# A linear-attention and token-mixing kernel: state update split over VectorE and GpSimd, mixing by single tiles and token pairs, weight flips ranked later, and a planner with larger latencies

## The chip, the cores and the metric

The kernel runs on one core of one Trainium2 chip. The metric is the device time of one execution in microseconds (us); lower is better. Fast runs of one kernel on one chip agree within about 1.5% here. The profile of the kernel before is of a run that the record marks slow (169.96 us, 0.1 us above the slowest fast run timed beside it). Ratios are the mean time of one kernel's fast runs over the mean of the other kernel's fast runs of the same rounds, so they are not quite the ratio of the medians that are quoted.

## The reference

Two stages follow each other. For each of 4 batches and 8 heads (768 tokens, head width 48) a recurrence runs over the tokens:

```python
for t in range(S):
    cur = einsum('bhd,bhe->bhde', u * k_t, v_t)
    y_t = einsum('bhd,bhde->bhe', r_t, state + cur)
    state = w[..., None] * state + einsum('bhd,bhe->bhde', k_t, v_t)
```

The result, as x with 384 channels per token, goes through a token-mixing layer:

```python
theta = x @ w_theta
yr = einsum('ts,bsd->btd', w_tok_r, x * cos(theta))
yi = einsum('ts,bsd->btd', w_tok_i, x * sin(theta))
u = x + yr + yi
out = u + maximum(u @ w_ch, 0)
```

The mixing of one output token needs all tokens s of its batch.

## The kernel before

The kernel records tasks first. A task has an engine, an expected duration, what it reads and writes, a priority and the PSUM banks that it takes. A list scheduler, run while the program is built, then fixes the order of the instructions on each engine. On the chip each engine works through its order and waits where data is late. The order depends on what the planner believes of delays:

```python
    def add(self, eng, ns, fn, rd=(), wr=(), prio=0.0, lat=60.0, ...):
        ...
    # in order(): a task has been chosen for engine e
                    free_at[e] = now + ns
                    t.end = now + ns + t.lat
                    ...
                    for x in t.users:
                        x.ready = max(x.ready, t.end)
```

The tokens are cut into 6 chunks of 128 per batch, worked in pairs (`pr`). The front of a batch turns r, k and v into scores, outputs and the running state. The state of chunk cc is made by four VectorE instructions, and GpSimd scales it to the bf16 operand of the next chunk:

```python
                    for hp in range(HP):
                        nc.vector.scalar_tensor_tensor(
                            Y[:, cc, hp, :], Y[:, cc - 1, hp, :], wC[:, hp:hp + 1],
                            src[:, hp], op0=Alu.mult, op1=Alu.add)
                ...
                P.add(POOL, ..., lambda cc=cc: nc.gpsimd.tensor_mul(Sb[:, cc], Y[:, cc], wide(wC, D)), ...)
```

The token weights are turned by TensorE (24 flips of three 128x128 blocks); ScalarE empties all 24 banks. The mixing takes two token tiles at a time, waits for all of the batch's zr and zi (`zk`), and flips both tiles together:

```python
        zk = [("zr", zj, o) for o in range(NCH)] + [("zi", zj, o) for o in range(NP)]
        for pr in range(NP):
            for t in range(2):
                for part in range(4):        # three matmuls each: WrT first, then WiT
                    P.add(PE, 495, mix, rd=zk + [...], ...)
                P.add(DVE, ..., un[:, t] = bank + x ...)
            flip6(uT ..., both tiles, ...)   # 6 transposes, one ScalarE eviction
            for t in range(2):
                P.add(PE, 495, chan, ...)    # channel matmuls
                P.add(DVE, ..., fin[:, t] = max(bank, 0) + un[:, t] ...)
            P.add(SP, 500, one output DMA for two tiles)
```

The fronts of later batches have higher priority than the mixing of earlier ones, so the mixing fills TensorE's gaps.

Of the kernel before, what the change touches and what calls it, by code (L numbers as in the profile page):

```python
# [29 lines left out]

class Task:
    __slots__ = ("eng", "ns", "fn", "deps", "prio", "seq", "lat", "acq", "uses", "nwait",
                 "users", "ready", "end", "mode")


class Plan:
# [9 lines left out]
    def add(self, eng, ns, fn, rd=(), wr=(), prio=0.0, lat=60.0, acq=(), use=(), mode=None):  # L46
        t = Task()
        t.eng, t.ns, t.fn, t.prio, t.lat, t.mode = eng, ns, fn, prio, lat, mode
# [23 lines left out]
    def order(self):  # L72
# [15 lines left out]
        while len(out) < n:  # L88
            for e in waiting:
                while free_at[e] <= now:  # L90
                    nfree = sum(1 for b in banks if b[0] <= now)
                    best = None
                    for t in waiting[e]:
                        if t.ready <= now and len(t.acq) <= nfree:
                            if best is None or (t.prio, t.seq) < (best.prio, best.seq):
                                best = t
# [13 lines left out]
                    t.end = now + ns + t.lat  # L110
# [6 lines left out]
                    for x in t.users:  # L117
                        x.ready = max(x.ready, t.end)
                        x.nwait -= 1
                        if x.nwait == 0:  # L120
                            waiting[x.eng].append(x)
# [19 lines left out]
def kernel(  # L141
# [63 lines left out]
    Ys = ring(1, [C, NS, HP, D], F32, "Y")  # L205
# [8 lines left out]
    uns = ring(2, [C, 2, HD], BF16, "un")  # L214
    uTs = ring(2, [C, 2, ND, C], BF16, "uT")
    fins = ring(2, [C, 2, HD], F32, "fin")
# [11 lines left out]
    def pool_ns(n):  # L228
        return 190 + 1.95 * n
# [112 lines left out]
    def token_weights(prio):  # L342
        for to in range(NCH):
            for src, dst, key in ((moe_w_tok_r, WrT, "WrT"), (moe_w_tok_i, WiT, "WiT")):
                i = load_rows(src[to * C:(to + 1) * C, :].rearrange("p (o c) -> p o c", o=2), 2)
                for sg in range(2):
# [10 lines left out]
                    def evac(sg=sg, tok=tok, dst=dst, to=to):  # L357
                        nc.scalar.activation(  # L358
                            dst[:, 3 * sg:3 * sg + 3, to * C:(to + 1) * C],
                            bank(tok)[:, :3 * C].rearrange("p (j c) -> p j c", j=3), Act.Copy)  # L360
                    P.add(ACT, act_ns(3 * C), evac, use=[tok], wr=[(key, to, sg)],
                          prio=prio + to)
# [15 lines left out]
    def front(b, base):  # L378
        Y, Sb = Ys[0], Sbs[b % 2]
        x, zr, zi = xs[b % 3], zrs[b % 2], zis[b % 2]  # L380
        xi, zj = b % 3, b % 2
        for pr in range(NP):
# [33 lines left out]
            for c in range(2):  # L416
# [12 lines left out]
                P.add(PE, 330, scores, rd=[kT, rT], acq=tk, prio=pb + 2, mode=1)  # L429
# [20 lines left out]
            P.add(ACT, 130, lambda td=td, dg=dg: nc.scalar.activation(  # L450
# [19 lines left out]
            for c in cs:  # L470
                cc = 2 * pr + c

                def update(cc=cc, c=c, ts=ts):
                    src = bank(ts)[:, c * HP * D:(c + 1) * HP * D].rearrange(
                        "p (h e) -> p h e", h=HP)
                    if cc == 0:
                        nc.vector.tensor_copy(Y[:, 0], src)
                        return
                    for hp in range(HP):
                        nc.vector.scalar_tensor_tensor(  # L480
                            Y[:, cc, hp, :], Y[:, cc - 1, hp, :], wC[:, hp:hp + 1],
                            src[:, hp], op0=Alu.mult, op1=Alu.add)
                P.add(DVE, 270 if cc == 0 else 480, update, use=[ts],
                      rd=["wC"] + ([("Y", cc - 1)] if cc else []), wr=[("Y", cc)], prio=pb + 2)
                P.add(POOL, pool_ns(HP * D), lambda cc=cc: nc.gpsimd.tensor_mul(  # L485
                    Sb[:, cc], Y[:, cc], wide(wC, D)),
                    rd=[("Y", cc), "wC"], wr=[("Sb", b % 2, cc)], prio=pb + 2)
# [29 lines left out]
            P.add(PE, 900, outputs, rd=[rT] + mk + [kv_] + [  # L517
# [14 lines left out]
            for t in range(2):  # L532
# [12 lines left out]
                P.add(ACT, act_ns(HD), lambda th=th: nc.scalar.activation(  # L545
# [5 lines left out]
            P.add(POOL, pool_ns(2 * HD), lambda sn=sn, pr=pr: nc.gpsimd.tensor_mul(  # L551
                zi[:, 2 * pr:2 * pr + 2], x[:, 2 * pr:2 * pr + 2], sn),
                rd=xk + [("sin", g % 2, t) for t in range(2)], wr=[("zi", zj, pr)], prio=pb + 9)


    def mixing(b, base):
        x, zr, zi = xs[b % 3], zrs[b % 2], zis[b % 2]
        xi, zj = b % 3, b % 2
        zk = [("zr", zj, o) for o in range(NCH)] + [("zi", zj, o) for o in range(NP)]
        for pr in range(NP):  # L560
            g = b * NP + pr
            un, uT, fin = uns[g % 2], uTs[g % 2], fins[g % 2]
            pb = base + 10 * pr
            for t in range(2):
                to = 2 * pr + t
                tm = ("mx", b, to)
                for part in range(4):
                    def mix(tm=tm, to=to, part=part):
                        WT, z = ((WrT, zr), (WiT, zi))[part // 2]
                        for j in range(3):  # L570
                            so = 3 * (part % 2) + j
                            nc.tensor.matmul(bank(tm)[:, :HD], WT[:, so, to * C:(to + 1) * C],  # L572
                                             z[:, so], start=(part == 0 and j == 0),
                                             stop=(part == 3 and j == 2))
                    P.add(PE, 495, mix, rd=zk + [(n, to, s) for n in ("WrT", "WiT") for s in (0, 1)],
                          acq=[tm] if part == 0 else [], use=[] if part == 0 else [tm],
                          wr=[] if part == 0 else [tm], prio=pb + 2 * t, mode=0)
                P.add(DVE, dve_ns(HD), lambda tm=tm, t=t, to=to, un=un: nc.vector.tensor_add(
                    un[:, t], bank(tm)[:, :HD], x[:, to]), use=[tm],
                    rd=[("x", xi, pr, hi) for hi in range(2)], wr=[("un", g % 2, t)],  # L580
                    prio=pb + 2 * t)
            flip6(uT.rearrange("p t d c -> p (t d) c"),
                  [un[:, t, dk * C:(dk + 1) * C] for t in range(2) for dk in range(ND)],
                  ("TU", b, pr), pb + 4, [("un", g % 2, t) for t in range(2)], [("uT", g % 2)])
            for t in range(2):
                tf = ("f", b, 2 * pr + t)

                def chan(tf=tf, t=t, uT=uT):
                    for dk in range(ND):
                        nc.tensor.matmul(bank(tf)[:, :HD], uT[:, t, dk, :], Wch[:, dk, :],  # L590
                                         start=(dk == 0), stop=(dk == ND - 1))
                P.add(PE, 495, chan, rd=[("uT", g % 2), ("Wch", 0), ("Wch", 2)], acq=[tf],
                      prio=pb + 4, mode=0)
                P.add(DVE, dve_ns(HD), lambda tf=tf, t=t, un=un, fin=fin:
                      nc.vector.scalar_tensor_tensor(fin[:, t], bank(tf)[:, :HD], 0.0, un[:, t],
                                                     op0=Alu.max, op1=Alu.add),
                      use=[tf], rd=[("un", g % 2, t)], wr=[("fin", g % 2, t)], prio=pb + 4)
            P.add(SP, 500, lambda fin=fin, pr=pr: nc.sync.dma_start(
                out=out[b, 2 * pr * C:(2 * pr + 2) * C, :].rearrange("(t p) n -> p t n", p=C),
                in_=fin), rd=[("fin", g % 2, t) for t in range(2)], wr=[("out", b, pr)],  # L600
                prio=-2e6, lat=2000)

    setup()
    square(moe_w_theta, Wth, "Wth", 20, 5.5)
    front(0, 0)
    token_weights(20)
# [39 lines left out]
```

## Time and profile before

| | before |
|---|---|
| time, median of 3 runs | 169.72 us (169.3 to 169.85) |
| span of the profiled run | 168.2 us |
| TensorE, VectorE, ScalarE, GpSimd busy | 136.4, 118.0, 90.0, 76.2 us |
| first mixing matmul starts | 49.9 us |
| batch 1's first outputs start (its matmuls with the scores) | 52.6 us |
| last theta group (the three theta matmuls of the last tile) starts | 136.1 us |

The page's lines of busy time in 40 equal slices (4.2 us each; a digit is tenths) show that the program has regimes:

```profile
PE   0354675999648997989979998989899899999960
...
DVE  2549369381479899997999699958999654443242
ACT  3673581999972766557953459327661481011110
...
PEclk9999997899999999999995999999999999999998
```

TensorE has gaps for the first third and hardly any in the last fifth; VectorE is fullest in the middle and thin in the last fifth. The same by window, with busy time and instruction count of each engine in each stretch:

```profile
0.00:53.00 53.00, 33.38 (x453) 26.75 (x453) 31.00 (x72) 36.08 (x67) 26.10 (x37) 0.97 0.98 244
30.00:45.00 15.00, 13.03 (x165) 11.38 (x164) 7.12 (x16) 15.00 (x36) 5.53 (x5) 0.98 1.04 288
53.00:136.50 83.50, 76.65 (x1019) 49.58 (x1014) 74.57 (x163) 47.97 (x79) 48.44 (x45) 0.98 0.54 119
136.50:168.20 31.70, 26.38 (x176) 15.36 (x174) 12.39 (x25) 5.93 (x10) 1.67 (x2) 0.98 0.20 76
```

The columns are the stretch, its length, then TensorE matmuls, weight loads, VectorE, ScalarE, GpSimd, then the granted TensorE clock, the DMA share and GB/s. TensorE idles 19.6 of the first 53 us and only 6.9 of the next 83.5. From 30 to 45 us ScalarE has no free moment. The chain of waits (start, length, what) in that stretch:

```profile
37.61 0.57 ACT WiT L358
...
39.88 0.67 ACT WrT L358
40.56 0.77 ACT WiT L358 x2
...
41.74 1.12 ACT WiT L358 x2
42.86 1.12 ACT Wch L338 x2
```

These are the weight evictions, L358.

### The profile page before, as it was taken

To read this page: it belongs to the slowest core of one execution; us is meant where nothing else is said; L and a number is where in the kernel's file an instruction comes from. 1 tells how busy PE (TensorE), PEld (TensorE's weight loads), DVE (VectorE), ACT (ScalarE), POOL (GpSimd) and SP (SyncE) were. 2 spreads that over 40 slices of the span, in tenths; PEclk is the share of its full clock that TensorE was granted. 3 is DMA by queue.
4 is the path that set the end of the run, shared out by engine and by line. 5 is a ranking of instruction groups with operands and counts; after the bars stand their busy time and mean duration, and the time that the engine had idled before them with its cause. 6 is when DMAs were issued, how large, how long until landed. Compare 5 with 4: busy or idle time off the path is not lost.

```text
span 168.2 us, 4181 instructions
## 1 busy us (share of the span) xinstructions
PE 136.4 (81%) x1641; PEld 91.7 (54%) x1641; DVE 118.0 (70%) x257; ACT 90.0 (53%) x155; POOL 76.2 (45%) x82
## 2 busy tenths in 40 slices
PE   0354675999648997989979998989899899999960
PEld 0243545879435655556765664556746555655530
DVE  2549369381479899997999699958999654443242
ACT  3673581999972766557953459327661481011110
POOL 6228247055298398927773774306517360000000
PEclk9999997899999999999995999999999999999998
DMA  4999999998999996099969972202200002220222
GB/s 88 222 236 218 214 264 383 410 339 172 180 215 208 194 207 124 0 228 194 243 167 213 218 156 44 97 2 93 97 0 4 0 4 93 93 77 17 97 95 93
DMA packets 80892, 25.25 MB, mean 150 GB/s; under 512 B 75368, under 2 KB 79336, under 8 KB 80872
## 3 DMA queue, kind: packets, MB, share of 16 engines
q1 hardware_dynamic: 80848, 24.98, 60.9%
q8 instruction: 13, 0.21, 0.5%
q14 instruction: 7, 0.06, 0.1%
q10 hardware_dynamic: 24, 0.00, 0.0%
HBM read 20.25 MB, written 4.72 MB: 148 GB/s over the span
## 4 chain that ended last, share of the span: by engine, by line
PE 38%; DVE 31%; ACT 15%; issue 6%; DMA 5%; POOL 2%; SPq 2%; DVEq 0%; POOLq 0%; ACTq 0%
PE bank_61 L572 3%; DVE Y_120 L480 3%; PE bank_66 L572 3%; DMA ld_86<-in_r_dram 3%; DVE Kw_98 L404 3%; PE bank_64 L572 2%; DMA ld_94<-in_r_dram 2%; PE bank_68 L572 2%; DVE PD_112 L437 2%; ACT KT_110 L373 2%; ACT WiT L358 2%; DVE zr_132 L548 2%; PE bank_63 L572 2%; ACT sin_136 L542 2%; DVE PD_113 L437 2%
## 5 line engine op out<-in xcount | busy, mean ns | idle before, releaser
L572 PEld LDWEIGHTS <-WrT 128*128 128x128 bf16 x144 | 14.0, 100 | 9.2 <-issue 0.9
L572 PEld LDWEIGHTS <-WiT 128*128 128x128 bf16 x144 | 12.9, 98 | 6.6
L485 POOL TENSOR_TENSOR Sb_122<-Y_120,wC 128x192 bf16<-128x192 f32 x10 | 6.1, 614 | 9.1 <-DVE Y_120 L480 8.4
L392 POOL TENSOR_TENSOR Rw_96<-ld_85,wpow 128x384 bf16<-128x384 f32 x6 | 5.9, 995 | 5.1 <-PE bank_67 L370 5.1
L485 POOL TENSOR_TENSOR Sb_121<-Y_120,wC 128x192 bf16<-128x192 f32 x10 | 5.7, 574 | 3.1 <-DVE Y_120 L480 2.3
L538 PEld LDWEIGHTS <-xT_138 128*128 128x128 bf16 x36 | 3.4, 107 | 5.6 <-ACT xT_138 L373 2.3
L551 POOL TENSOR_TENSOR zi_134<-x_129,sin_136 128x768 bf16<-128x768 bf16 x2 | 3.3, 1635 | 6.8 <-ACT sin_136 L542 6.8
L404 DVE TENSOR_TENSOR Kw_100<-ld_86,wpinv 128x384 bf16<-128x384 f32 x6 | 5.7, 963 | 0.0
L373 ACT ACTIVATE uT_143<-bank_62 128x768 bf16<-128x768 bf16 x2 | 1.6, 812 | 7.5 <-PE bank_62 L370 7.5
L392 POOL TENSOR_TENSOR Rw_95<-ld_94,wpow 128x384 bf16<-128x384 f32 x4 | 4.3, 1074 | 2.9 <-DMA ld_94<-in_r_dram 2.9
L373 ACT ACTIVATE uT_142<-bank_63 128x768 bf16<-128x768 bf16 x2 | 1.6, 811 | 7.1 <-PE bank_63 L370 7.1
L590 PEld LDWEIGHTS <-uT_143 128*128 128x128 bf16 x36 | 3.1, 98 | 4.1 <-ACT uT_143 L373 2.5
L548 DVE TENSOR_TENSOR zr_132<-bank_68,x_129 128x384 bf16<-128x384 f32 x3 | 1.7, 554 | 5.1 <-ACT bank_68 L545 2.7
L392 POOL TENSOR_TENSOR Rw_95<-ld_88,wpow 128x384 bf16<-128x384 f32 x4 | 4.7, 1188 | 1.0 <-PE bank_63 L370 1.0
L551 POOL TENSOR_TENSOR zi_134<-x_131,sin_136 128x768 bf16<-128x768 bf16 x2 | 3.3, 1636 | 3.9 <-ACT sin_136 L542 2.7
L538 PEld LDWEIGHTS <-xT_139 128*128 128x128 bf16 x36 | 3.1, 98 | 3.5 <-ACT xT_139 L373 1.9
L426 PEld LDWEIGHTS <-KT_111 64*128 64x128 bf16 x96 | 3.0, 101 | 3.6 <-ACT KT_111 L373 2.2
L426 PEld LDWEIGHTS <-KT_110 64*128 64x128 bf16 x96 | 3.1, 101 | 3.3 <-ACT KT_110 L373 2.3
L590 PEld LDWEIGHTS <-uT_142 128*128 128x128 bf16 x36 | 3.2, 97 | 3.1 <-ACT uT_142 L373 1.4
L551 POOL TENSOR_TENSOR zi_135<-x_130,sin_137 128x768 bf16<-128x768 bf16 x2 | 3.3, 1637 | 3.5 <-ACT sin_137 L542 3.2
L274 PE MATMUL bank_61<-ident_f,wu 8*128 8x8 f32 x1 | 0.2, 241 | 5.6 <-DMA wu<-in_u_dram 5.6
L437 DVE TENSOR_TENSOR PD_112<-RT_106,KT_110 128x1024 bf16<-128x1024 bf16 x3 | 2.6, 875 | 2.9 <-ACT KT_110 L373 2.9
(561 smaller groups left out, 504.4 us busy)
## 6 DMA issues: line engine op xcount, KB each, us to landing
out_dram<-fin_144 SPq DMA_DIRECT2D x6, 384.0 KB, 2.5
out_dram<-fin_145 SPq DMA_DIRECT2D x6, 384.0 KB, 2.8
ld_85<-in_r_dram SPq DMA_DIRECT2D x6, 192.0 KB, 4.3
ld_86<-in_k_dram SPq DMA_DIRECT2D x6, 192.0 KB, 3.6
ld_87<-in_v_dram SPq DMA_DIRECT2D x6, 192.0 KB, 3.5
ld_88<-in_r_dram SPq DMA_DIRECT2D x4, 192.0 KB, 4.4
ld_89<-in_k_dram SPq DMA_DIRECT2D x4, 192.0 KB, 4.6
ld_90<-in_v_dram SPq DMA_DIRECT2D x4, 192.0 KB, 3.6
```

The source lines that it names most:

```text
L373: P.add(ACT, act_ns(n * C), lambda: nc.scalar.activation(dst, bank16(tok)[:, :n * C].rearrange("p (a c) -> p a c", a=n), Act.Copy), use=[t ...
L392: lambda c=c, vec=vec, Rw=Rw, ir=ir: vec.tensor_mul(Rw[:, c, :, :D], Ls[ir][:, c * HD:(c + 1) * HD].rearrange("p (h d) -> p h d", h=H), wpow),
L404: P.add(DVE, dve_ns(HD), lambda c=c, Kw=Kw, ik=ik: nc.vector.tensor_mul(Kw[:, c, :, :D], Ls[ik][:, c * HD:(c + 1) * HD].rearrange("p (h d) ...
L426: nc.tensor.matmul(bank(tk[hi])[:, hp * C:(hp + 1) * C], KT[q, c, hp, :], RT[q, c, hp, :], start=(hp == 0), stop=(hp == HP - 1))
L437: nc.vector.tensor_mul(PD, RT, KT)
L480: nc.vector.scalar_tensor_tensor(Y[:, cc, hp, :], Y[:, cc - 1, hp, :], wC[:, hp:hp + 1], src[:, hp], op0=Alu.mult, op1=Alu.add)
L485: P.add(POOL, pool_ns(HP * D), lambda cc=cc: nc.gpsimd.tensor_mul(Sb[:, cc], Y[:, cc], wide(wC, D)), rd=[("Y", cc), "wC"], wr=[("Sb", b % ...
L538: nc.tensor.matmul(bank(th)[:, :HD], xT[:, t, dk, :], Wth[:, dk, :], start=(dk == 0), stop=(dk == ND - 1))
L548: P.add(DVE, dve_ns(HD), lambda th=th, to=to: nc.vector.tensor_mul(zr[:, to], bank(th)[:, :HD], x[:, to]), use=[th], rd=xk, wr=[("zr", zj, ...
L551: P.add(POOL, pool_ns(2 * HD), lambda sn=sn, pr=pr: nc.gpsimd.tensor_mul(zi[:, 2 * pr:2 * pr + 2], x[:, 2 * pr:2 * pr + 2], sn), rd=xk + [ ...
L572: nc.tensor.matmul(bank(tm)[:, :HD], WT[:, so, to * C:(to + 1) * C], z[:, so], start=(part == 0 and j == 0), stop=(part == 3 and j == 2))
L590: nc.tensor.matmul(bank(tf)[:, :HD], uT[:, t, dk, :], Wch[:, dk, :], start=(dk == 0), stop=(dk == ND - 1))
```

## The change

Its intent is to relieve VectorE of the state update and ScalarE of half the evictions, to let the mixing of a batch begin before its last pair is ready and drain tile by tile, to keep the weights from delaying the first batch, and to give the planner more realistic numbers. The diff, cut to its core:

```diff
+LATENCY = {PE: 200.0, DVE: 150.0, ACT: 175.0, POOL: 160.0, SP: 2200.0}
-    def add(..., lat=60.0, ...):
+        t.lat = LATENCY[eng] if lat is None else lat
-                    t.end = now + ns + t.lat
+                    done = now + ns
+                    t.end = done + t.lat
-                        x.ready = max(x.ready, t.end)
+                        x.ready = max(x.ready, done if x.eng == e else t.end)
 # ... state update
-                    for hp in range(HP):
-                        nc.vector.scalar_tensor_tensor(Y[:, cc, hp, :], ...)
+                        nc.vector.tensor_add(Ys[cc % 2], src, Zs[(cc - 1) % 2])
+                P.add(POOL, ..., nc.gpsimd.tensor_mul(Zs[cc % 2], Ys[cc % 2], wide(wC, D)))
+                P.add(ACT, ..., nc.scalar.activation(Sb[:, cc], Zs[cc % 2], Act.Copy))
 # ... weight evictions
-                        nc.scalar.activation(...)
+                        if sg: nc.vector.tensor_copy(o, i)
+                        else:  nc.scalar.activation(o, i, Act.Copy)
 # ... mixing: one tile at a time, three parts, each with the four matmuls of one token pair
+        for to in range(NCH):
+            for part in range(NP):
+                P.add(PE, 660, mix, rd=[(n, zj, 2 * part + j) for n in ("zr", "zi") for j in range(2)] + [...])
+            # then add, a flip of 3 blocks, channel matmuls, relu-add, output DMA for this tile
 # ... ranks
-    square(moe_w_theta, Wth, "Wth", 20, 5.5)
+    square(moe_w_theta, Wth, "Wth", 15, 8.5)
-    token_weights(20)
+    token_weights(60)
```

Some expected durations were corrected too, the planner no longer adds 100 ns for a change of TensorE mode around weight flips, zi is made per tile instead of per pair, and un, uT and fin rotate over three buffers.

More of the change, by code (lines that the diff above doesn't have):

```diff
@@ L28 @@
 PE, DVE, ACT, POOL, SP = "PE", "DVE", "ACT", "POOL", "SP"
+KEEP = 0
+LATENCY = {PE: 200.0, DVE: 150.0, ACT: 175.0, POOL: 160.0, SP: 2200.0}
 class Task:
     __slots__ = ("eng", "ns", "fn", "deps", "prio", "seq", "lat", "acq", "uses", "nwait",
-                 "users", "ready", "end", "mode")
+                 "users", "ready", "end", "mode", "keep")
 class Plan:
@@ L44, in __init__, with add @@
         self.bank_of = {}
-    def add(self, eng, ns, fn, rd=(), wr=(), prio=0.0, lat=60.0, acq=(), use=(), mode=None):
+    def add(self, eng, ns, fn, rd=(), wr=(), prio=0.0, lat=None, acq=(), use=(), mode=0, keep=0):
         t = Task()
-        t.eng, t.ns, t.fn, t.prio, t.lat, t.mode = eng, ns, fn, prio, lat, mode
+        t.eng, t.ns, t.fn, t.prio, t.mode = eng, ns, fn, prio, mode
+        t.keep = keep
+        t.lat = LATENCY[eng] if lat is None else lat
         t.seq = len(self.tasks)
@@ L93, in order @@
                     for t in waiting[e]:
-                        if t.ready <= now and len(t.acq) <= nfree:
+                        if t.ready <= now and (
+                                not t.acq or len(t.acq) + t.keep <= nfree):
                             if best is None or (t.prio, t.seq) < (best.prio, best.seq):
@@ L204 @@
     mATs = ring(6, [C, 2, HP, C], BF16, "mAT")
-    Ys = ring(1, [C, NS, HP, D], F32, "Y")
+    Ys = ring(2, [C, HP, D], F32, "Y")
+    Zs = ring(2, [C, HP, D], F32, "Z")
     Sbs = ring(2, [C, NS, HP, D], BF16, "Sb")
@@ L213 @@
     xTs = ring(2, [C, 2, ND, C], BF16, "xT")
-    uns = ring(2, [C, 2, HD], BF16, "un")
-    uTs = ring(2, [C, 2, ND, C], BF16, "uT")
-    fins = ring(2, [C, 2, HD], F32, "fin")
+    uns = ring(3, [C, HD], BF16, "un")
+    uTs = ring(3, [C, ND, C], BF16, "uT")
+    fins = ring(3, [C, HD], F32, "fin")
     Wth = sb.tile([C, ND, HD], BF16, name="Wth")
@@ L357, in evac @@
                     def evac(sg=sg, tok=tok, dst=dst, to=to):
-                        nc.scalar.activation(
-                            dst[:, 3 * sg:3 * sg + 3, to * C:(to + 1) * C],
-                            bank(tok)[:, :3 * C].rearrange("p (j c) -> p j c", j=3), Act.Copy)
-                    P.add(ACT, act_ns(3 * C), evac, use=[tok], wr=[(key, to, sg)],
-                          prio=prio + to)
+                        o = dst[:, 3 * sg:3 * sg + 3, to * C:(to + 1) * C]
+                        i = bank(tok)[:, :3 * C].rearrange("p (j c) -> p j c", j=3)
+                        if sg:
+                            nc.vector.tensor_copy(o, i)
+                        else:
+                            nc.scalar.activation(o, i, Act.Copy)
+                    P.add(DVE if sg else ACT, dve_ns(3 * C) if sg else act_ns(3 * C), evac,
+                          use=[tok], wr=[(key, to, sg)], prio=prio + to)
     def flip6(dst, blocks, tok, prio, rd, wr):
@@ L378, in front @@
     def front(b, base):
-        Y, Sb = Ys[0], Sbs[b % 2]
+        Sb = Sbs[b % 2]
         x, zr, zi = xs[b % 3], zrs[b % 2], zis[b % 2]
@@ L428, in scores @@
                                              start=(hp == 0), stop=(hp == HP - 1))
-                P.add(PE, 330, scores, rd=[kT, rT], acq=tk, prio=pb + 2, mode=1)
+                P.add(PE, 345, scores, rd=[kT, rT], acq=tk, prio=pb + 2, mode=1)
                 for hi in range(2):
@@ L449, in front @@
             P.add(PE, 200, diag, rd=[kP, "uw"], acq=[td], prio=pb + 4, mode=0)
-            P.add(ACT, 130, lambda td=td, dg=dg: nc.scalar.activation(
+            P.add(ACT, 70, lambda td=td, dg=dg: nc.scalar.activation(
                 dg, bank(td)[:, :2 * H], Act.Copy), use=[td], wr=[kd], prio=pb + 4)
@@ L476, in update @@
                     if cc == 0:
-                        nc.vector.tensor_copy(Y[:, 0], src)
-                        return
-                    for hp in range(HP):
-                        nc.vector.scalar_tensor_tensor(
-                            Y[:, cc, hp, :], Y[:, cc - 1, hp, :], wC[:, hp:hp + 1],
-                            src[:, hp], op0=Alu.mult, op1=Alu.add)
-                P.add(DVE, 270 if cc == 0 else 480, update, use=[ts],
-                      rd=["wC"] + ([("Y", cc - 1)] if cc else []), wr=[("Y", cc)], prio=pb + 2)
-                P.add(POOL, pool_ns(HP * D), lambda cc=cc: nc.gpsimd.tensor_mul(
-                    Sb[:, cc], Y[:, cc], wide(wC, D)),
-                    rd=[("Y", cc), "wC"], wr=[("Sb", b % 2, cc)], prio=pb + 2)
+                        nc.vector.tensor_copy(Ys[0], src)
+                    else:
+                        nc.vector.tensor_add(Ys[cc % 2], src, Zs[(cc - 1) % 2])
+                P.add(DVE, 270, update, use=[ts], rd=[("Z", (cc - 1) % 2)] if cc else [],
+                      wr=[("Y", cc % 2)], prio=pb + 2)
+                P.add(POOL, pool_ns(HP * D) - 70, lambda cc=cc: nc.gpsimd.tensor_mul(
+                    Zs[cc % 2], Ys[cc % 2], wide(wC, D)),
+                    rd=[("Y", cc % 2), "wC"], wr=[("Z", cc % 2)], prio=pb + 2)
+                P.add(ACT, act_ns(HP * D, False), lambda cc=cc: nc.scalar.activation(
+                    Sb[:, cc], Zs[cc % 2], Act.Copy),
+                    rd=[("Z", cc % 2)], wr=[("Sb", b % 2, cc)], prio=pb + 2)
             ty = [("y", b, pr, hi) for hi in range(2)]
@@ L516, in outputs @@
                             first[hi] = False
-            P.add(PE, 900, outputs, rd=[rT] + mk + [kv_] + [
+            P.add(PE, 720, outputs, rd=[rT] + mk + [kv_] + [
                 ("Sb", b % 2, 2 * pr + c - 1) for c in range(2) if 2 * pr + c > 0],
@@ L544, in front @@
                     prio=pb + 8)
-                P.add(ACT, act_ns(HD), lambda th=th: nc.scalar.activation(
+                P.add(ACT, 465, lambda th=th: nc.scalar.activation(
                     bank(th)[:, :HD], bank(th)[:, :HD], Act.Sin, bias=pi2), use=[th],
@@ L550, in front @@
                     wr=[("zr", zj, to)], prio=pb + 9)
-            P.add(POOL, pool_ns(2 * HD), lambda sn=sn, pr=pr: nc.gpsimd.tensor_mul(
-                zi[:, 2 * pr:2 * pr + 2], x[:, 2 * pr:2 * pr + 2], sn),
-                rd=xk + [("sin", g % 2, t) for t in range(2)], wr=[("zi", zj, pr)], prio=pb + 9)
+                P.add(POOL, pool_ns(HD), lambda sn=sn, to=to, t=t: nc.gpsimd.tensor_mul(
+                    zi[:, to], x[:, to], sn[:, t]),
+                    rd=xk + [("sin", g % 2, t)], wr=[("zi", zj, to)], prio=pb + 9)
     def mixing(b, base):
@@ L558, in mixing @@
         xi, zj = b % 3, b % 2
-        zk = [("zr", zj, o) for o in range(NCH)] + [("zi", zj, o) for o in range(NP)]
-        for pr in range(NP):
-            g = b * NP + pr
-            un, uT, fin = uns[g % 2], uTs[g % 2], fins[g % 2]
-            pb = base + 10 * pr
-            for t in range(2):
-                to = 2 * pr + t
-                tm = ("mx", b, to)
-                for part in range(4):
-                    def mix(tm=tm, to=to, part=part):
-                        WT, z = ((WrT, zr), (WiT, zi))[part // 2]
-                        for j in range(3):
-                            so = 3 * (part % 2) + j
-                            nc.tensor.matmul(bank(tm)[:, :HD], WT[:, so, to * C:(to + 1) * C],
-                                             z[:, so], start=(part == 0 and j == 0),
-                                             stop=(part == 3 and j == 2))
-                    P.add(PE, 495, mix, rd=zk + [(n, to, s) for n in ("WrT", "WiT") for s in (0, 1)],
-                          acq=[tm] if part == 0 else [], use=[] if part == 0 else [tm],
-                          wr=[] if part == 0 else [tm], prio=pb + 2 * t, mode=0)
-                P.add(DVE, dve_ns(HD), lambda tm=tm, t=t, to=to, un=un: nc.vector.tensor_add(
-                    un[:, t], bank(tm)[:, :HD], x[:, to]), use=[tm],
-                    rd=[("x", xi, pr, hi) for hi in range(2)], wr=[("un", g % 2, t)],
-                    prio=pb + 2 * t)
-            flip6(uT.rearrange("p t d c -> p (t d) c"),
-                  [un[:, t, dk * C:(dk + 1) * C] for t in range(2) for dk in range(ND)],
-                  ("TU", b, pr), pb + 4, [("un", g % 2, t) for t in range(2)], [("uT", g % 2)])
-            for t in range(2):
-                tf = ("f", b, 2 * pr + t)
-                def chan(tf=tf, t=t, uT=uT):
-                    for dk in range(ND):
-                        nc.tensor.matmul(bank(tf)[:, :HD], uT[:, t, dk, :], Wch[:, dk, :],
-                                         start=(dk == 0), stop=(dk == ND - 1))
-                P.add(PE, 495, chan, rd=[("uT", g % 2), ("Wch", 0), ("Wch", 2)], acq=[tf],
-                      prio=pb + 4, mode=0)
-                P.add(DVE, dve_ns(HD), lambda tf=tf, t=t, un=un, fin=fin:
-                      nc.vector.scalar_tensor_tensor(fin[:, t], bank(tf)[:, :HD], 0.0, un[:, t],
-                                                     op0=Alu.max, op1=Alu.add),
-                      use=[tf], rd=[("un", g % 2, t)], wr=[("fin", g % 2, t)], prio=pb + 4)
-            P.add(SP, 500, lambda fin=fin, pr=pr: nc.sync.dma_start(
-                out=out[b, 2 * pr * C:(2 * pr + 2) * C, :].rearrange("(t p) n -> p t n", p=C),
-                in_=fin), rd=[("fin", g % 2, t) for t in range(2)], wr=[("out", b, pr)],
-                prio=-2e6, lat=2000)
@@ new lines, in mixing, with mix, chan @@
+        for to in range(NCH):
+            g = b * NCH + to
+            pr = to // 2
+            un, uT, fin = uns[g % 3], uTs[g % 3], fins[g % 3]
+            pb = base + 5 * to
+            tm, tf = ("mx", b, to), ("f", b, to)
+            for part in range(NP):
+                def mix(tm=tm, to=to, part=part):
+                    for j in range(2):
+                        so = 2 * part + j
+                        for i, (WT, z) in enumerate(((WrT, zr), (WiT, zi))):
+                            nc.tensor.matmul(bank(tm)[:, :HD], WT[:, so, to * C:(to + 1) * C],
+                                             z[:, so], start=(so == 0 and i == 0),
+                                             stop=(so == NCH - 1 and i == 1))
+                P.add(PE, 660, mix,
+                      rd=[(n, zj, 2 * part + j) for n in ("zr", "zi") for j in range(2)]
+                      + [(n, to, s) for n in ("WrT", "WiT") for s in (0, 1)],
+                      acq=[tm] if part == 0 else [], use=[] if part == 0 else [tm],
+                      wr=[] if part == 0 else [tm], prio=pb, keep=KEEP)
+            P.add(DVE, dve_ns(HD), lambda tm=tm, to=to, un=un: nc.vector.tensor_add(
+                un, bank(tm)[:, :HD], x[:, to]), use=[tm],
+                rd=[("x", xi, pr, hi) for hi in range(2)], wr=[("un", g % 3)], prio=pb)
+            flip6(uT, [un[:, dk * C:(dk + 1) * C] for dk in range(ND)],
+                  ("TU", b, to), pb + 1, [("un", g % 3)], [("uT", g % 3)])
+            def chan(tf=tf, uT=uT):
+                for dk in range(ND):
+                    nc.tensor.matmul(bank(tf)[:, :HD], uT[:, dk, :], Wch[:, dk, :],
+                                     start=(dk == 0), stop=(dk == ND - 1))
+            P.add(PE, 495, chan, rd=[("uT", g % 3), ("Wch", 0), ("Wch", 2)], acq=[tf],
+                  prio=pb + 1)
+            P.add(DVE, dve_ns(HD), lambda tf=tf, un=un, fin=fin:
+                  nc.vector.scalar_tensor_tensor(fin, bank(tf)[:, :HD], 0.0, un,
+                                                 op0=Alu.max, op1=Alu.add),
+                  use=[tf], rd=[("un", g % 3)], wr=[("fin", g % 3)], prio=pb + 1)
+            P.add(SP, 300, lambda fin=fin, to=to: nc.sync.dma_start(
+                out=out[b, to * C:(to + 1) * C, :], in_=fin), rd=[("fin", g % 3)],
+                wr=[("out", b, to)], prio=-2e6, lat=2000)
```

## The prediction

> **What bounds the kernel now.** The page gives TensorE 136.4 us of 168.2 (81%), VectorE 118.0, ScalarE 90.0, GpSimd 76.2. These sums hide three stages (busy time by window):
>
> - 0 to 53 us (batch 1's first outputs): TensorE busy 33.4. From 30 to 45 us ScalarE is busy 15.0 of 15: it empties 24 weight-flip banks (562 to 686 ns, 0.37 us apart), and the chain of waits runs over these, then over xT, sin and KT to 48 us. VectorE is busy 7.1 of those 15. Mixing starts at 49.9 us, because it waits for all of batch 0's zr and zi.
> - 53 to 136.5 us: VectorE busy 74.6 of 83.5, TensorE 76.7. The chain is mostly VectorE.
> - 136.5 us to the end: TensorE back to back (3 matmuls each 0.49 us), then 7 us of drain.
>
> **The change, costed.**
>
> 1. State update: 64 scalar_tensor_tensor (259 ns; four take 0.70 us of VectorE) become 16 adds of 128x192, estimate 0.28 each (the existing 192-wide copy takes 0.26 to the next start). VectorE saves 6.7 us, 5.5 of it in the middle stage. GpSimd's multiply (0.5 to 0.6 us) enters the recurrence, and ScalarE gets 20 casts[...]. A step of the recurrence grows from 0.7 to about 1.3 us; outputs wait one ScalarE hop longer. With five steps in over 20 us a batch this hides, except at the start (1 to 2 us).
>    [...]
> 2. Half of the weight evictions move to VectorE: 12 x about 0.45 us, where it has 8 us spare; ScalarE loses 12 x 0.37 = 4.4 us of chain.
> 3. Mixing by token pair: TensorE work equal (288 matmuls at 0.163 us). In the instruction order, when batch 1's first outputs are issued, 48 mixing and 9 channel matmuls are done instead of 12 and 0: 7.4 us of TensorE work moved into early idle time. From there to the last outputs 116 mixing matmuls remain instead of 153. Three tiles' mixing adds and relu-adds (2.8 us of VectorE) leave the middle too.
> 4. Wth loads later: pair 1's k and v land some 1.5 us sooner.
> 5. [...] Mixing holds banks earlier; with 8 this can stall the front.
> 6. Tail: after the last theta 96 mixing and 30 channel matmuls remain instead of 108 and 36, 2.9 us less; draining one tile saves about 1 us.
>
> **Sum.** Start: about even (gains of 2 and 4 spent on the work moved in and longer hops). Middle: VectorE loses 5.5 + 2.8 us, so 83 becomes 75. Tail: 31.7 becomes 28. Span about 156.5; timed runs read 1.5 us more: **158 us**, 8 times in 10 within 152 to 165. Faster by over 2%: 0.91; within 2%: 0.07; slower: 0.02.
>
> **What would show it.** VectorE total about equal but near 66 us in the middle; the update near 0.28 us; first mixing at about 35 us; no run of ScalarE evictions on the chain at 37 to 44 us; last theta near 128 us.
>
> **What would make it wrong.** TensorE waiting for Sb (through GpSimd and ScalarE); banks held by half-finished mixing; loads stuck behind output DMAs in SP's queue; or, for a larger gain, realistic latencies in the ordering removing waits everywhere.

The sum: the start about even at some 53 us, the middle 75, the tail 28, a span of about 156.5 us and 158 us timed. What the trace of before shows: the 24 VectorE adds that write x, with one input in PSUM, took 0.540 to 0.557 us beside a GpSimd instruction and 0.541 to 0.549 alone; the Kw multiply, with two inputs in SBUF, took 0.54 to 0.56 us alone and up to 1.99 beside one. The evictions took 0.50 to 0.75 us each (562 to 686 ns are means of groups), "about 0.45 us" is near the 0.46 us from one 384-wide VectorE instruction that reads PSUM to the next, and the 1.5 us of step 4 and the 1.3 us of a step of the recurrence are estimates (the second Wth load held SP's queue for 1.50 us).

## The result, and the profile after

The changed kernel takes 159.54 us (median of 4 runs, 159.03 to 159.89) against 169.51 us for the kernel before in the same rounds: ratio 0.9411, 95% interval 0.9375 to 0.9446. The prediction was 158 us within 152 to 165.

```profile
PE   0347789999999979988958999899999999999971
...
DVE  5449796896657999999998899977999956434441
ACT  3593576886955569785846576938935475212120
...
PEclk9999999999999999999995699999999999999999
```

A slice is now 3.9 us. TensorE is nearly full from the seventh slice on; the deepest dent is at the 21st, with a low granted clock in the two slices after it. By window:

```profile
0.00:53.00 53.00, 41.06 (x484) 30.76 (x485) 38.34 (x73) 35.21 (x64) 27.39 (x41) 1.00 0.93 236
30.00:45.00 15.00, 14.79 (x151) 11.84 (x150) 11.11 (x24) 10.89 (x23) 7.07 (x8) 1.00 1.03 298
53.00:136.50 83.50, 77.76 (x1045) 51.91 (x1043) 74.54 (x135) 54.39 (x104) 51.64 (x54) 0.96 0.60 134
136.50:157.80 21.30, 16.92 (x116) 10.15 (x114) 8.06 (x15) 3.44 (x7) 0.00 (x0) 0.99 0.20 75
```

| milestone (us) | before | after |
|---|---|---|
| second pair's scores start | 22.4 | 18.7 |
| third pair's outputs start | 41.7 | 35.9 |
| first mixing matmul | 49.9 | 34.5 |
| batch 1's first outputs | 52.6 | 53.8 |
| last theta group starts | 136.1 | 130.4 |
| end of the span | 168.2 | 157.8 |

The account closes on TensorE. Its number of matmuls is the same (1641) and its busy time nearly so (136.4 and 135.7 us), so the span can fall only by the idle time. In the first 53 us the idle time fell from 19.6 to 11.9 us, 7.7 of the 10.4 us of span. The rest is 1.1 us in the next stretch (6.85 to 5.74), 0.9 in the last (5.3 to 4.4) and 0.7 of busy time. The 7.7 us is the work moved forward: batch 1's first outputs come no earlier than before, but 48 mixing and 9 channel matmuls stand before them in the order, instead of 12 and 0. That moving work forward is not enough by itself is seen below, in the run with the mixing alone.

The chain in the stretch that had been ScalarE's:

```profile
33.98 0.33 PE bank_64 L361 x3
34.31 0.33 PE bank_66 L361 x3
34.64 0.65 PE bank_65 L582 x4
35.29 0.33 PE bank_61 L361 x3
```

Weight flips (L361) follow each other at TensorE's own pace, and a mixing part (L582, four matmuls in 0.65 us) already stands between them. The state update is one instruction now; count, then minimum, median and maximum in ns of two of its groups:

```profile
L491 DVE TENSOR_TENSOR Y_121<-bank_64,Z_122 x3: 341/342/348, 22.3 to 110.6; 128x192 f32<-128x192 f32 x3
L491 DVE TENSOR_TENSOR Y_120<-bank_68,Z_123 x2: 344/346/348, 57.7 to 90.3; 128x192 f32<-128x192 f32 x2
```

In all, the update's VectorE busy time fell from 12.5 to 5.5 us.

### The profile page after: what moved, and what is told of

Read it like the earlier page. It is cut to its first block, busy times and chain, and to the rows that moved or that the text cites. A ratio compares the mean times of both kernels' runs of the same rounds, so it can differ in the third digit from the quotient of the medians.

```text
span 157.8 us, 4220 instructions
## 1 busy us (share of the span) xinstructions
PE 135.7 (86%) x1641; PEld 92.8 (59%) x1641; DVE 120.9 (77%) x221; ACT 93.0 (59%) x175; POOL 79.0 (50%) x94
## 4 chain that ended last, share of the span: by engine, by line
PE 56%; DVE 22%; ACT 7%; issue 6%; DMA 5%; SPq 1%; POOL 0%; ACTq 0%; DVEq 0%; POOLq 0%
PE bank_64 L582 7%; PE bank_66 L582 5%; PE bank_62 L582 5%; PE bank_65 L582 4%; DMA ld_90<-in_v_dram 3%; DMA ld_86<-in_r_dram 3%; DVE Kw_98 L416 3%; DVE PD_113 L449 2%; DVE mAT_115 L443 2%; PE bank_63 L582 2%; DVE zr_136 L560 2%; PE bank_67 L382 2%; DVE mAT_116 L443 2%; PE bank_61 L382 2%; DVE Kw_97 L416 1%
## 5 line engine op out<-in xcount | busy, mean ns | idle before, releaser
L582 PEld LDWEIGHTS <-WrT 128*128 128x128 bf16 x144 | 14.3, 99 | 7.6 <-issue 0.3
L582 PEld LDWEIGHTS <-WiT 128*128 128x128 bf16 x144 | 14.3, 99 | 7.3 <-issue 0.3
L494 POOL TENSOR_TENSOR Z_122<-Y_120,wC 128x192 f32<-128x192 f32 x12 | 6.1, 507 | 12.8 <-DVE Y_120 L491 6.5
L563 POOL TENSOR_TENSOR zi_137<-x_132,sin_139 128x384 bf16<-128x384 bf16 x4 | 3.7, 943 | 9.9 <-ACT sin_139 L554 9.9
L494 POOL TENSOR_TENSOR Z_123<-Y_121,wC 128x192 f32<-128x192 f32 x8 | 5.3, 663 | 5.3 <-DVE Y_121 L491 5.3
L582 PE MATMUL bank_64<-zr_135,WrT 128*128 128x384 bf16 x18 | 5.9, 327 | 0.0
L582 PE MATMUL bank_64<-zi_137,WiT 128*128 128x384 bf16 x18 | 5.9, 326 | 0.0
L582 PE MATMUL bank_62<-zr_136,WrT 128*128 128x384 bf16 x18 | 5.9, 326 | 0.0
L582 PE MATMUL bank_62<-zi_138,WiT 128*128 128x384 bf16 x18 | 5.9, 326 | 0.0
L582 PE MATMUL bank_64<-zr_136,WrT 128*128 128x384 bf16 x18 | 5.9, 326 | 0.0
L582 PE MATMUL bank_64<-zi_138,WiT 128*128 128x384 bf16 x18 | 5.9, 326 | 0.0
L582 PE MATMUL bank_66<-zi_137,WiT 128*128 128x384 bf16 x18 | 5.9, 326 | 0.0
L582 PE MATMUL bank_66<-zr_135,WrT 128*128 128x384 bf16 x18 | 5.8, 325 | 0.0
L550 PEld LDWEIGHTS <-xT_141 128*128 128x128 bf16 x36 | 3.7, 107 | 3.3 <-issue 1.4
L449 DVE TENSOR_TENSOR PD_112<-RT_106,KT_110 128x1024 bf16<-128x1024 bf16 x3 | 3.3, 1092 | 2.6 <-ACT KT_110 L385 2.6
L563 POOL TENSOR_TENSOR zi_138<-x_132,sin_140 128x384 bf16<-128x384 bf16 x4 | 3.6, 910 | 2.6 <-ACT sin_140 L554 2.6
L563 POOL TENSOR_TENSOR zi_137<-x_134,sin_139 128x384 bf16<-128x384 bf16 x4 | 3.6, 910 | 2.4 <-ACT sin_139 L554 2.4
L550 PEld LDWEIGHTS <-xT_142 128*128 128x128 bf16 x36 | 3.4, 97 | 2.3 <-ACT xT_142 L385 0.2
```

The source lines that it names most:

```text
L449: nc.vector.tensor_mul(PD, RT, KT)
L494: P.add(POOL, pool_ns(HP * D) - 70, lambda cc=cc: nc.gpsimd.tensor_mul(Zs[cc % 2], Ys[cc % 2], wide(wC, D)), rd=[("Y", cc % 2), "wC"], wr= ...
L550: nc.tensor.matmul(bank(th)[:, :HD], xT[:, t, dk, :], Wth[:, dk, :], start=(dk == 0), stop=(dk == ND - 1))
L563: P.add(POOL, pool_ns(HD), lambda sn=sn, to=to, t=t: nc.gpsimd.tensor_mul(zi[:, to], x[:, to], sn[:, t]), rd=xk + [("sin", g % 2, t)], wr= ...
L582: nc.tensor.matmul(bank(tm)[:, :HD], WT[:, so, to * C:(to + 1) * C], z[:, so], start=(so == 0 and i == 0), stop=(so == NCH - 1 and i == 1))
```

## The experiments

Twelve kernels ran, all with correct results, four to a chip. The kernel before was run beside each four. Times are medians of fast runs; after ran at 0.9411 of before, and as a control on a third chip at 0.9408.

| run | what | us | ratio to before (95%) |
|---|---|---|---|
| e1_planner_only | before + new latencies | 171.13 | 1.0097 (1.0046 to 1.0148) |
| e2_planner_old | after - new latencies | 164.26 | 0.9686 (0.9632 to 0.9741) |
| e3_stt_same_order | after, old update in the same order | 162.56 | 0.9587 (0.9529 to 0.9645) |
| e4_gate_all | after, mixing waits for the whole batch | 161.66 | 0.9545 (0.9484 to 0.9605) |
| e5_evict_act | after, all evictions on ScalarE | 159.98 | 0.9415 (0.9321 to 0.9509) |
| e6_update_old | after, old update, replanned | 161.96 | 0.9512 (0.9423 to 0.9601) |
| e7_lat_minus10 | after, latencies 10% smaller | 158.38 | 0.9314 (0.9251 to 0.9376) |
| e8_outs_last | after, output DMAs behind all loads | 160.12 | 0.9419 (0.9353 to 0.9485) |
| e9_after_again | after, unchanged (control) | 159.49 | 0.9408 (0.9353 to 0.9463) |
| e10_mixing_only | before + new mixing | 170.22 | 1.0051 (0.9990 to 1.0112) |
| e11_mixing_planner | before + new mixing + new latencies | 163.58 | 0.9659 (0.9591 to 0.9728) |
| e12_lat_plus10 | after, latencies 10% larger | 158.43 | 0.9347 (0.9262 to 0.9431) |

Differences given below in percent are differences of these ratios; 1% is 1.7 us.

### The planner's latencies alone, on the kernel before

```diff
-    def add(..., lat=60.0, ...)
+        t.lat = LATENCY[eng] if lat is None else lat
-                        x.ready = max(x.ready, t.end)
+                        x.ready = max(x.ready, done if x.eng == e else t.end)
```

> Before, with only the planner's new latencies and its rule that a task behind its own engine waits no latency; no instruction is added or removed, only the order changes. Theory A (the prediction: the parts of the work itself bring the 10 us, the ordering only a remainder): 166 to 169.5 us, less than a third of the gain. Rival B (the better latencies in the ordering bring most of it): 160 to 164 us.

Measured 171.13 us, 1.0% slower than before; neither theory had expected a loss. No instruction differs, only the order. The last theta group moved from 136.1 to 139.4 us, and the time from there to the end fell from 32.2 to 29.9 us, so the loss lies before it. Taken alone, the better numbers bring nothing to the old kernel. Why this order is worse was not followed further.

### The planner's old latencies, in the kernel after

```diff
-        t.lat = LATENCY[eng] if lat is None else lat
+        t.lat = 60.0 if lat is None else lat
-                        x.ready = max(x.ready, done if x.eng == e else t.end)
+                        x.ready = max(x.ready, t.end)
```

> After, with the old planner latencies (60 ns everywhere, on the own engine too). Theory A: it loses at most 3 us, 160 to 163 us. Rival B: most of the gain goes, 165 us or more.

Measured 164.26 us: 2.8% lost, 4.7 us, just under rival B's line and well over the 3 us of theory A. In the changed kernel the latencies and the rule for a task behind its own engine, which this run takes back together, matter; the two were not tested apart. The traces say where. The last theta group starts at 130.8 us here and at 130.4 in after; from there after needs 27.4 us and this one 31.7. Of the 4.3 us, 1.3 are 8 more mixing matmuls left to do (104 instead of 96). Most of the other 3.0 us is a repeated stall: 30 channel matmuls are left in both, so ten tiles, and six of them in a row (139.8 to 157.4 us) lose about 0.34 us each as the next two fences show, some 2 us; earlier tiles lose less, and the rest was not traced tile by tile. The chain of waits of this run, over one tile and a bit, with its flip (L382), mixing parts (L582) and channel matmuls (L598):

```profile
142.74 0.34 PE bank L382 x3
143.08 0.65 PE bank L582 x4
143.73 0.64 PE bank L598 x3
144.37 1.30 PE bank L582 x8
...
145.68 0.34 PE bank L382 x3
```

The same of after:

```profile
142.65 0.17 PE bank_67 L382 x3
142.81 1.30 PE bank_62 L582 x8
144.11 0.49 PE bank_68 L598 x3
144.60 0.65 PE bank_64 L582 x4
145.25 0.17 PE bank_61 L382 x3
```

A tile takes 2.94 us here and 2.60 in after, with the same 18 matmuls. The flip takes 0.34 instead of 0.17 us and the channel matmuls 0.64 instead of 0.49: each has a wait in it. Its timeline gives the reason:

```profile
144.70 0.33 PE L582 MATMUL bank<-zi,WiT 128*128 128x384 bf16 x1
...
145.06 0.56 DVE L590 TENSOR_TENSOR un<-bank,x 128x384 bf16<-128x384 f32 x1
...
145.67 0.17 PEld L382 LDWEIGHTS <-un 128*128 128x128 bf16 x3 [0.39 <-DVE un L590]
...
146.10 0.49 ACT L385 ACTIVATE uT<-bank 128x384 bf16<-128x384 bf16 x1 [2.45 <-PE bank L382]
...
146.64 0.28 PEld L598 LDWEIGHTS <-uT 128*128 128x128 bf16 x3 [0.37 <-ACT uT L385]
```

The tile's last mixing matmul was issued at 144.70 us, so TensorE was free of it at 144.86. The add could start at 145.06 and the flip at 145.67: 0.81 us, 0.56 of it the add itself, of which one mixing part (0.65 us) covers most, but not all. The old planner believed in 60 + 475 + 60 = 595 ns for that path (its own numbers for the add and two latencies), less than the 660 it allows for a part, and so put one part between. The new numbers, 200 + 475 + 150 = 825 ns, make it put channel matmuls and a part there. From the flip to the channel matmuls it is the same: 0.80 us from the flip's last issue (145.85) to 146.65, covered by one part in this order and by two in after. The order is fixed, so what the planner gets wrong by 0.15 us is paid again at each of these tiles (0.34 against 0.17 us at the flip, 0.64 against 0.49 at the channel matmuls).

### The old update at the same places

```diff
-                        nc.vector.tensor_add(Ys[cc % 2], src, Zs[(cc - 1) % 2])
+                        for hp in range(HP):
+                            nc.vector.scalar_tensor_tensor(
+                                Ys[cc % 2][:, hp, :], Ys[(cc - 1) % 2][:, hp, :], wC[:, hp:hp + 1],
+                                src[:, hp], op0=Alu.mult, op1=Alu.add)
```

> After, with every instruction in its place on every engine, but each of the 16 state adds replaced by the old four scalar_tensor_tensor (the recurrence then no longer waits for GpSimd; GpSimd and ScalarE still make Z and Sb). Adds 16 x about 0.42 = 6.7 us of VectorE. Theory A (VectorE is the limit of the middle stage): 3 to 6 us slower than after, 162.5 to 165.5 us, all of it between batch 1's first outputs and the last theta. Rival C (TensorE is the limit there, VectorE's relief was swallowed): less than 1.5 us, under 161 us.

Measured 162.56 us, 1.8% or 3.0 us over after, at the low edge of theory A (its 162.5 us). The last theta group starts at 134.0 us instead of 130.4, and the time from there to the end is 27.4 us in both. So the loss lies before the last theta, as expected. The old update costs 6.9 us more of VectorE than the new one, but VectorE's busy time between batch 1's first outputs and the end of the last theta rose only from 71.0 to 74.5 us, because the Kw multiplies (VectorE's weighting of k) got shorter (17.0 us in the whole run instead of 20.3; they overlap GpSimd's instructions for 9.5 us instead of 14.4). That stretch grew from 77.2 to 80.2 us, so nearly all of the VectorE time that was really added was lost, as theory A has it.

### The mixing gated on the whole batch

```diff
-                      rd=[(n, zj, 2 * part + j) for n in ("zr", "zi") for j in range(2)]
+                      rd=[(n, zj, o) for n in ("zr", "zi") for o in range(NCH)]
```

> After, but each part of the mixing waits for all of the batch's zr and zi again (single tiles and pair parts kept), replanned. Theory A: the first mixing matmul moves from 34.5 to about 48 us, the 7 us of work that filled the early idle time comes back later: 3 to 6 us slower than after, 162.5 to 165.5 us. Rival B: under 161 us.

Measured 161.66 us, 1.3% or 2.3 us over after, less than theory A's 3 us and more than rival B's line by 0.7 us. The first mixing matmul came at 40.5 us, not at 48: the first batch finishes earlier in the changed kernel anyway. So the early start by token pair is worth about 2 us, of which the scatter of a redrawn order (1 to 1.6 us, see below) may be a good part; the rest of the work that moved forward moves without the gate by pair (40 mixing matmuls still stand before batch 1's first outputs, 48 in after).

### All evictions on ScalarE

```diff
-                        if sg: nc.vector.tensor_copy(o, i)
-                        else:  nc.scalar.activation(o, i, Act.Copy)
+                        nc.scalar.activation(o, i, Act.Copy)
```

> After, with all 24 weight-flip evictions on ScalarE again, replanned. Theory A (the eviction chain of 12 x 0.37 us on ScalarE was worth 2 to 4 us of the start): 161.5 to 163.5 us. Rival D (with the flips ranked behind the first batch and mixing able to start after the first of them, the evictions no longer bind): within 1 us of after, 158.5 to 160.5 us.

Measured 159.98 us over three fast runs (a fourth, 161.83 us, was slow and is left out), a ratio of 0.9415 against 0.9411: no difference. Rival D holds. This run's window from 30 to 45 us shows why (the profile is of the slow run; only its shares are used):

```profile
30.00:45.00 15.00, 14.93 (x151) 11.92 (x150) 5.68 (x12) 14.47 (x36) 6.66 (x8) 1.00 0.99 289
```

ScalarE is as full as in before (14.47 of 15 us), and TensorE is full as well (14.93). In the changed kernel the evictions are in nobody's way that can be measured, with mixing parts at hand to stand between the flips. The chain of waits in before did run over them; whether they held that kernel back was not tested, since no run split the evictions there.

### The old update, replanned

```diff
-                        nc.vector.tensor_add(Ys[cc % 2], src, Zs[(cc - 1) % 2])
-                # GpSimd: Z = Y * wC; ScalarE: Sb = bf16(Z)
+                        nc.vector.scalar_tensor_tensor(Y[:, cc, hp, :], ...)   # four
+                # GpSimd: Sb = Y * wC
```

> After, with the whole state update as before (four scalar_tensor_tensor on VectorE, GpSimd writes Sb straight, no ScalarE cast), replanned. From the run with the same order, where the four instructions cost 3.0 us: 162 to 163.5 us if order and work add up. Rival E (the shorter path to Sb gives back what VectorE loses): 159 to 161 us.

Measured 161.96 us, a ratio 1.0% over that of after, 1.7 us, with an interval of about 0.9% either way. That lies between the two expectations. With the run at the same order (3.0 us) it puts the update's worth at 1.7 to 3 us; the 1.7 is about as large as the scatter that the next two runs show.

### Two redrawn orders

```diff
-LATENCY = {PE: 200.0, DVE: 150.0, ACT: 175.0, POOL: 160.0, SP: 2200.0}
+LATENCY = {PE: 180.0, DVE: 135.0, ACT: 158.0, POOL: 144.0, SP: 2200.0}   # e7
+LATENCY = {PE: 220.0, DVE: 165.0, ACT: 192.0, POOL: 176.0, SP: 2200.0}   # e12
```

> After, with the planner's latencies cut by a tenth (180, 135, 158, 144 ns): no instruction differs, the order is drawn anew. A measure of how much a redrawn order moves the time by chance: if within 0.5 us of after, effects of 2 us in the other runs can be read as effects of the part; if 1.5 us or more, only larger ones can.

> After, with the planner's latencies raised by a tenth (220, 165, 192, 176 ns): a second draw of the order. If it too is about 1 us off the control in either direction, the scatter of a redrawn order is about 1 us; theory A has no other expectation.

Measured 158.38 and 158.43 us, 1.0% and 0.6% better than after by the ratios. Both directions are a little faster, so this is the scatter of a redrawn order, about 1 to 1.6 us, and differences of 1 us between replanned kernels (e4, e5, e6, e8) can't be read. Both also beat before and after, but their intervals touch or overlap those of after; they were not shown to be better by more than chance.

TensorE's clock may be part of the scatter. The mean granted clock of the runs of after was 0.979, of e7 0.997. In the trace of after TensorE stands still for 1.9 us, from 79.9 to 81.8 us, waiting for a product on VectorE, and then:

```profile
81.00:82.00 1.00, 0.20 (x8) 0.21 (x8) 1.00 (x2) 0.00 (x0) 1.00 (x2) 1.00 0.96 185
82.00:83.00 1.00, 1.00 (x28) 0.93 (x26) 1.00 (x1) 0.18 (x1) 1.00 (x1) 0.68 0.18 37
83.00:84.00 1.00, 0.49 (x5) 0.33 (x4) 1.00 (x2) 0.47 (x1) 1.00 (x2) 0.50 0.99 198
...
88.00:89.00 1.00, 1.00 (x8) 0.67 (x6) 1.00 (x3) 0.00 (x0) 0.36 (x1) 0.50 1.14 229
89.00:90.00 1.00, 1.00 (x26) 0.67 (x25) 0.47 (x2) 0.64 (x1) 1.00 (x2) 0.90 1.06 210
```

From 82.4 to 89.2 us the granted clock is 0.50, and four mixing matmuls take 1.28 us on the chain instead of 0.65. These 7 us cost up to 3.5 us (an estimate: half of the 7 us, since the mixing matmuls take twice as long there). But the profile of before has as much of it (27.1 to 30.5 and 88.5 to 91.9 us at 0.50), so it does not explain the gain of after over before:

```profile
85.10:88.50 3.40, 2.44 (x55) 1.92 (x50) 3.40 (x13) 1.69 (x2) 2.44 (x4) 1.00 0.59 170
88.50:91.90 3.40, 3.40 (x16) 1.92 (x16) 3.40 (x10) 1.54 (x2) 0.53 (x2) 0.50 1.10 212
```

No long standstill came before the second of these: from 85.1 to 88.5 us TensorE was busy 2.44 us and never idle for more than 0.52 us at a stretch. What brings the half clock about was not isolated. Nor does the clock separate the redrawn orders: in e12 TensorE stands still for 2.91 us, and then four mixing matmuls (84.1 to 85.6 us) take 0.48 to 0.53 us each where they take 0.33 before and later. The granted clock of e12's profiled run was 0.984, of e7's 0.993, and the two are about as fast (158.43 and 158.38 us). What makes them faster than after was not isolated.

### Output DMAs behind all loads

```diff
-                wr=[("out", b, to)], prio=-2e6, lat=2000)
+                wr=[("out", b, to)], prio=2e6, lat=2000)
-    fins = ring(3, [C, HD], F32, "fin")
+    fins = ring(12, [C, HD], F32, "fin")
```

> After, with the output DMAs ranked last on SP's queue (behind all loads) and 12 output tiles instead of 3, so that no load stands behind an output that is not yet computed (in the profile of after SP waits 14 us in one case and 57 us in all for outputs). Theory F (loads held up behind outputs delay batches 1 and 2): 1 to 3 us faster than after, 156.5 to 158.5 us. Rival G (the loads have room enough with 12 slots): within 1 us.

Measured 160.12 us, 0.1% from after: rival G. SP's long waits for outputs (up to 14.0 us in the trace of after) do not hold the changed kernel. In before the DMA share was 0.00 from 66 to 72 us behind such a wait; whether that cost before anything was not tested.

### The mixing, without and with the latencies, and the control

```diff
 # e10: before, with the mixing function and the un, uT, fin rings of after (zi still made by pairs)
 # e11: the same, with the latencies and the own-engine rule of e1
```

> The changed kernel unaltered, as the control on this chip for the three runs beside it: 159 to 160.5 us.

> Before, with the new mixing alone (single tiles, parts by token pair, three rotating buffers) under the old planner latencies. Theory H (single tiles leave less slack between add, flip, eviction and channel matmul, so they need an order that knows the real delays): little or nothing, 167 to 170 us, with the last stage's tiles 2.9 us apart as in the run with the old latencies. Rival I (the mixing brings its gain by itself): 165 us or less.

> Before, with the new mixing and the new planner latencies, but the old state update, the old evictions and the old ranks. Theory H: the latencies, which cost 1.7 us on the old mixing, now gain 3 to 5 us over the run with the mixing alone, 163 to 166 us. Rival I: within 1.5 us of the mixing alone.

The control read 159.49 us, within its expectation and 0.05 us from the first chip. The mixing alone read 170.22 us (ratio 1.005, its interval includes 1): the largest part of the change, taken alone, brings nothing. With the latencies it read 163.58 us, 3.4% faster than before. Theory H holds, and the gain of the latencies on the new mixing (3.9%) is larger than it expected. The chain of the mixing alone near its end (flip L370, mixing L570, channel L586):

```profile
149.26 0.34 PE bank L370 x3
149.60 0.65 PE bank L570 x4
150.25 0.64 PE bank L586 x3
150.90 1.30 PE bank L570 x8
...
152.20 0.34 PE bank L370 x3
```

It has the 2.94 us per tile again. And with the latencies:

```profile
143.29 0.17 PE bank L376 x3
143.46 1.30 PE bank L576 x8
144.76 0.49 PE bank L592 x3
145.25 0.17 PE bank L376 x3
```

Here flip and channel matmuls are back at 0.17 and 0.49 us. The time from the last theta group to the end is 32.0 us with the mixing alone, as in before (32.2), and 28.0 with the latencies. The mixing alone has 44 mixing matmuls before batch 1's first outputs, nearly as many as after (48), but these outputs start at 55.8 us instead of 52.6: the work was moved forward, and nothing was gained by it. So the three ratios are: latencies alone 1.010, mixing alone 1.005, both 0.966. The two parts do not add; their interaction is 4.9% (1.010 + 1.005 - 1 - 0.966), 8 us.

## Why the prediction was right, and where it was not

**The total** (158 predicted, 159.5 measured) and the mechanism on TensorE held: equal work, the early idle time filled, batch 1's first outputs at about the same time (52.6 and 53.8 us; "Start: about even"), the first mixing at 34.5 us (35 predicted), the tail shorter. Its parts missed by 1 to 2 us in both directions (the middle long, the tail short), so the closeness of the sum owes something to chance. The counts read from the order of instructions carried this, and they were right because that order already held the effect of every part, the planner's numbers too.

**Step 3** credited to "Mixing by token pair" what that part does not do alone. The mixing alone gave nothing, and with the latencies 3.4%. The prediction named realistic latencies only as what might make the gain larger. The runs showed them to be the condition of it: in the orders planned with 60 ns, single tiles leave one part of 0.65 us where the path needs 0.81; both orders planned with the larger delays cover it. The gate by pair itself is worth about 2 us.

**Step 2** failed: "ScalarE loses 12 x 0.37 = 4.4 us of chain". Putting the evictions back cost nothing that can be told from zero. The chain of before ran over them, but in the changed kernel TensorE has other work at hand there. The first sum took "gains of 2 and 4"; the 4 came from elsewhere. The second pair's scores started 3.7 us sooner (22.4 to 18.7), where step 4 said 1.5 for their loads. The runs divide this: with the latencies alone (e1) they start at 19.3 us, with everything but the latencies (e2) at 20.9. The third pair's outputs (41.7 to 35.9) are at 36.7 in e2 and at 41.8 in e11, so they come sooner by parts that e11 lacks: ranks, evictions, the update. The ranks were not undone by themselves. What remains between e11 (163.58) and the control (159.49), 4.1 us, holds the update (1.7 to 3 us), the ranks, the evictions and the zi halves together.

**Step 1**, right in kind, was mis-sized. The update's instruction takes 0.342 us and the next one starts 0.26 us after it, near the 0.28 expected. In the windows after 53 us the update's busy time fell from 8.6 to 3.8 us (5.5 expected off). But VectorE between batch 1's first outputs and the last theta went only from 75.0 to 71.0 us, not to 66: its other instructions grew. Over the whole run the Kw multiply rose from 18.9 to 20.3 us and the RT x KT product from 9.6 to 11.3. Both have two SBUF inputs; the product takes 0.68 us at best and up to 1.48. In this trace most of them were longer beside a GpSimd instruction, and the adds, with one input in PSUM, were not: all 16 adds took 0.340 to 0.349 us, 7 of them beside a GpSimd instruction; of the 24 Kw multiplies, the 7 that meet no GpSimd instruction took 0.54 to 0.56 us and the other 17 up to 1.82, 14 of them over 0.72 (in before 0.54 to 0.56 alone, up to 1.99 beside GpSimd). GpSimd is busy 79.0 us of a shorter span, where it was 76.2, and the Kw multiplies overlap its instructions for 14.4 us, where it was 11.8; I take this as the reason for the growth, which no run isolated. The cast took 0.36 us. The longer recurrence never showed: in the table of waits TensorE's matmuls waited 1.3 us in all for Sb.

**The middle** took 77.2 us from batch 1's first outputs to the end of the last theta, 75 predicted; the half clock at 82 to 89 us alone could be the difference, which was not tested. **The tail**, from the start of the last theta group, fell from 32.2 to 27.4 us, 4.8 where 3.7 was expected.

None of the fears came true except the last, the planner's numbers: waits for Sb stayed small and SP's queue did not matter (e8); whether banks were ever short was not looked at.

## What to carry to other kernels

When work is cut finer, the slack between dependent instructions shrinks with it; an order fixed in advance must then know the real delay from the end of one engine's work to the start of the next, or it pays the error at every piece (here 2.94 instead of 2.60 us for each of six tiles). Undo the parts of a change one at a time and also add them one at a time: here two parts were each worth nothing alone and 3.4% together. A busy engine on the chain of waits is not proof of a limit: here TensorE had other work at hand in the changed kernel, and giving ScalarE all the evictions back cost nothing that could be measured (e5: ScalarE busy 14.47 of 15 us, 0.9415 against 0.9411).
